# Attention, then two MoE layers, on one core: a unit's scores behind the preceding unit's values, and a last phase on three pairs of 512 tokens

## The chip, the core and the metric

The kernel runs on one core of one Trainium2 chip. A time is the device time of one execution in microseconds (us). TensorE (PE in the profile) does the matrix products, VectorE (DVE) and ScalarE (ACT) element-wise work, GpSimd (POOL) some of the same, and SyncE (SP) issues DMA transfers. PEld is the loading of TensorE's stationary operand; SPq is SP's instruction queue.

## What is computed

The inputs are float64 where the weights are concerned and float32 else. Attention over chunks of 32 queries: each chunk sees 16 tokens to its left, itself, 8 to its right, and 8 memory tokens. Behind it stand two feed-forward layers over 3072 tokens of width 512.

```python
for c in range(768 // 32):
    q_c = q[:, :, 32 * c:32 * c + 32]                       # 4 x 8 heads, 64 wide
    k_full = concat([mem_k, k[:, :, max(0, 32 * c - 16):32 * c + 40]])
    v_full = concat([mem_v, v[:, :, max(0, 32 * c - 16):32 * c + 40]])
    a = softmax(q_c @ k_full.T / 8)
    out[:, :, 32 * c:32 * c + 32] = a @ v_full
x = out.transpose(0, 2, 1, 3).reshape(3072, 512)
h = x @ w_in                                                # 512 -> 2048
x = (max(h, 0) + log1p(exp(-abs(h)))) @ w_out               # 2048 -> 512
return ((x @ w_a) * (x @ w_b)) @ w_o2                       # 512 -> 1536 -> 512
```

## The kernel before

**Products in three parts.** Every float32 operand of a wide product is kept as a high and a low part; a product is high x high, high x low and low x high, added up in PSUM. That makes three matmuls of each.

**First layer: 8 tiles of TT = 384 tokens.** A tile runs 16 blocks f of the hidden width. `emit_h` (L531) makes ph, 12 matmuls of 384 columns, in one of two PSUM banks of tag h. `emit_soft` (L543) forms the softplus: three ScalarE operations on e (L545 abs, L546 exp, L547 ln), one VectorE operation g (L549), then `split` into g_h and g_l. `emit_x1` (L555), two blocks later (LAG = 2), adds g times the second weight into four PSUM banks acc0 to acc3, 12 matmuls px. At a tile's end the four sums are copied and stored into x1_scratch.

**Attention in between.** 128 tokens with all heads are a unit; three units make a tile, and they are done while the tile before runs. Units 0 to 2 (tile 0) are done as blocks of 64 tokens ahead of everything, units 3 to 5 by a way of their own (EARLY_STEPS). Units u = 6 to 23, which the change touches, go through these steps of `class Unit` (L393):

- `turn` (L403): three VectorE transposes (L410, L412, L413) that bring the loaded keys kn and queries qn into kt and qt, and two small ScalarE copies of the memory keys into kt; for the first unit of a batch (u = 6, 12, 18) a small transpose of the memory keys ahead.
- `scores` (L417): 16 small float32 matmuls sc, which the profile shows as 32, into the two banks of tag att.
- `soft` (L432): maximum on VectorE, exponentials on ScalarE. `norm` (L440): the division, mostly on GpSimd.
- `flip` and `flip2` (L443): five VectorE transposes each, pieces 0 and 1 and then pieces 2 and 3 of af.
- `values` (L468): 16 such matmuls pxa, again 32 in the profile, the first half on pieces 0 and 1, the second on pieces 2 and 3, into one bank of tag att.
- `place` (L479): the result split into the x of the next tile, by ScalarE and VectorE (L484).

**What sets the order.** A table gives each step a place in slots, relative to the unit's place; two slots are one block f. `att_at(slot)` (L899) runs all steps that are due: at an even slot 2f behind ph and the softplus of block f, at an odd one behind the px matmuls. In tiles 1 to 6 the order of SP, TensorE and VectorE is the written one, ScalarE and GpSimd are ordered by a scheduler; in tile 0 and from tile 7 all are as written. Each instruction waits by semaphores for the data and for the free buffer it needs.

```python
STEPS = ((-8, "turn"), (-5.2, "scores"), (-4.9, "soft"), (-3, "norm"), (-0.9, "flip"), (1.1, "flip2"),
         (3, "values"), (3.1, "place"))
at = 2 * NF1 * (i + 1) // UPT - START + NEXT_LATER * (i == EARLY) - (i % UPT == UPT - 1)
plan += [(at + d - steps[-1][0], i, getattr(unit, step)) for d, step in steps]
```

The last unit of a tile (u = 8, 11, 14, 17, 20, 23) stands one slot earlier; `Loaded.fetch` (L184, issues L187 and L189), which loads the next tile's keys and queries in 4 parts of 8 or more DMAs, is planned 1 to 4 slots behind that unit's `turn`. Between these steps the raw weights of the second MoE are loaded and put together on VectorE (`Early`, val L640 and L641) and stored into v_scratch (L644).

**Last phase: the second layer on 4 pairs of 2 x 384 tokens.** For each of 12 blocks f, `pair_step` (L767) forms (x w_a) and (x w_b) of both halves by seven block products (Strassen's way: PRODUCTS = 11, s2, s3, s1, 12, 22, s4, on sums of quarters of x that `add_pair` makes), each product six matmuls of 384 columns (`product`, L720) into the banks pX, pY, pW, pV. VectorE adds and multiplies the results into c1 and c2, ScalarE and VectorE split them, and `job` (L739) multiplies 128 tokens of them with w_o2: six matmuls py of 512 columns, three jobs in a step. The sums of x are split into high and low by `split_hi` and `split_lo`, those of the first pair on VectorE during tile 7, those of the others during the preceding pair, mostly in its last step. From the second pair on, the weights' sums u are reloaded from u_scratch.

## Time and profile before

| what | value |
| --- | --- |
| median of three runs | 1189.16 us (1187.32 to 1193.07) |
| profiled execution, span of its instructions | 1185.4 us (its own time outside the span is not given) |
| TensorE busy | 1177.1 us, 99%, 7966 matmuls |
| loading of its operands | 1115.2 us, 94%, beside the matmuls |
| VectorE busy | 734.8 us, 62%, 1707 instructions |
| ScalarE busy | 537.0 us, 45%, 1329 instructions |
| GpSimd busy | 279.5 us, 24%, 249 instructions |

The profiled execution is one execution; its span ends 3.8 us below the median of the three timed runs. In the timeline, a row is a run of equal instructions: its start in us from the span's start, the time from its first start to its last end, the engine, the line, the operation, the tiles written and read with the shape, and the number of instructions. What stands in brackets is idle time of the engine ahead of it, and what ended it. Matmuls overlap, so the time that a group of them takes is read from its start to the start of the next group.

### The profile page before, as it was taken

Reading aid. Unit: us, or ns where it says so; the run is one execution under the profiler, and the core shown is the slowest. Engines: PE = TensorE matmul, PEld = TensorE weight load, DVE = VectorE, ACT = ScalarE, POOL = GpSimd, SP = SyncE. Lnnn points to the kernel's source line nnn. Section 1 sums busy time; section 2 is a strip of 40 time slices with the busy share of each in tenths; the row PEclk is TensorE's granted clock in tenths of the full one; section 3 lists DMA queues with packets and bytes.
Section 4 is the critical chain, followed back from the end, with each engine's and each line's share of the span. In section 5 each row is a group of like instructions: output and inputs, shape, how many; then the busy total and the mean of one; then the engine's idle time right before and its main releaser. Section 6 shows DMA issues by size and latency. Waiting matters only on the chain.

```text
span 1185.4 us, 21520 instructions
## 1 busy us (share of the span) xinstructions
PE 1177.1 (99%) x7966; PEld 1115.2 (94%) x7966; DVE 734.8 (62%) x1707; ACT 537.0 (45%) x1329; POOL 279.5 (24%) x249
## 2 busy tenths in 40 slices
PE   9999999999999999999999999999999999999998
PEld 7899999999999999999999999999999999999997
DVE  6888654555556555465387668755666456655565
ACT  6899565655656566565564433221112211212010
POOL 2000323223232222322325778200211002100000
PEclk9999999999999999999999999999999999999999
DMA  9955334353343633432556895788554965379521
GB/s 237 295 178 111 109 86 110 93 115 107 87 107 93 120 107 84 104 97 62 178 205 238 324 341 190 267 327 298 199 196 141 375 234 183 133 255 369 194 80 54
DMA packets 198841, 209.86 MB, mean 177 GB/s; under 512 B 121632, under 2 KB 150224, under 8 KB 198736
## 3 DMA queue, kind: packets, MB, share of 16 engines
q1 hardware_dynamic: 198352, 208.43, 54.9%
q8 instruction: 63, 1.03, 0.4%
q14 instruction: 42, 0.34, 0.1%
q0 software_dynamic: 384, 0.05, 0.0%
HBM read 158.11 MB, written 50.33 MB: 176 GB/s over the span
## 4 chain that ended last, share of the span: by engine, by line
PE 93%; ACT 3%; DVE 2%; DMA 1%; issue 1%; SPq 0%; DVEq 0%; ACTq 0%
PE ph L538 21%; PE px L562 21%; PE py L749 17%; PE pW L726 8%; PE pX L726 8%; PE pV L726 8%; PE pY L726 4%; PE pxa L476 2%; PE sc L429 1%; DMA raw<-in_moe_w_in_dram 1%; DVE tmp L122 1%; ACT sm L383 1%; DMA vv<-in_v_dram 0%; ACT work L383 0%; DVE tmp L121 0%
## 5 line engine op out<-in xcount | busy, mean ns | idle before, releaser
L538 PE MATMUL ph<-x,w 128*128 128x384 f32 x1536 | 289.7, 336 | 0.1
L538 PEld LDWEIGHTS ph<-x,w 128*128 128x128 f32 x1536 | 266.7, 188 | 2.2 <-issue 0.3
L749 PE MATMUL py<-w2o,c 128*128 128x512 f32 (+1 forms) x870 | 222.2, 392 | 0.0
L549 DVE SCALAR_TENSOR_TENSOR g<-ph,e 128x384 f32<-128x384 f32 x128 | 71.3, 557 | 205.6 <-ACT e L547 205.3
L749 PEld LDWEIGHTS py<-w2o,c 128*128 128x128 f32 x870 | 160.5, 188 | 25.3
L808 ACT CAST c<-c 128x384 fp32r<-128x384 f32 x48 | 24.7, 514 | 302.4 <-DVE c L806 269.8
L726 PE MATMUL pX<-x,u 128*128 128x384 f32 x576 | 115.5, 334 | 0.0
L758 DVE TENSOR_TENSOR y<-py,y 128x512 f32<-128x512 f32 (+1 forms) x121 | 83.0, 686 | 47.3 <-PE py L749 46.9
L545 ACT ACTIVATE e<-ph 128x384 f32<-128x384 f32 x128 | 62.3, 486 | 103.9 <-PE ph L538 89.9
L726 PEld LDWEIGHTS pX<-x,u 128*128 128x128 f32 x576 | 102.1, 188 | 4.1
L447 DVE STREAM_TRANSPOSE af<-sm 32x256 f32<-32x256 f32 x180 | 78.2, 435 | 2.5
L804 DVE TENSOR_TENSOR d<-pW,q 128x384 f32<-128x384 f32 x48 | 26.7, 557 | 68.5 <-PE pW L726 68.5
L546 ACT ACTIVATE e<-e 128x384 f32<-128x384 f32 x128 | 67.3, 526 | 4.0
L547 ACT ACTIVATE e<-e 128x384 f32<-128x384 f32 x128 | 67.3, 526 | 3.8
L383 ACT ACTIVATE sm<-sm,st 128x96 f32<-128x96 f32 x168 | 60.5, 362 | 3.6 <-DVE st L379 3.6
L818 ACT CAST c<-c 128x384 fp32r<-128x384 f32 x48 | 24.6, 513 | 77.9 <-DVE c L816 76.9
L726 PE MATMUL pW<-xs,u 128*128 128x384 f32 x288 | 57.8, 335 | 0.0
L726 PE MATMUL pV<-xx,u 128*128 128x384 f32 x288 | 57.8, 335 | 0.0
L726 PE MATMUL pV<-xs,u 128*128 128x384 f32 x288 | 57.6, 334 | 0.0
L726 PE MATMUL pY<-xs,u 128*128 128x384 f32 x288 | 57.6, 334 | 0.0
L726 PE MATMUL pW<-xx,u 128*128 128x384 f32 x288 | 57.6, 334 | 0.0
L726 PEld LDWEIGHTS pV<-xx,u 128*128 128x128 f32 x288 | 51.5, 188 | 4.1
(251 smaller groups left out, 2229.3 us busy)
## 6 DMA issues: line engine op xcount, KB each, us to landing
u<-u_scratch SPq DMA_DIRECT2D x108, 512.0 KB
u_scratch<-u SPq DMA_DIRECT2D x36, 512.0 KB
w2o<-w2o_scratch SPq DMA_DIRECT2D x36, 512.0 KB
u<-u_scratch SPq DMA_DIRECT2D x36, 256.0 KB
raw<-in_moe_w_in_dram SPq DMA_DIRECT2D x16, 512.0 KB
raw<-in_moe_w_out_dram SPq DMA_DIRECT2D x16, 512.0 KB
vn<-in_v_dram SPq DMA_DIRECT2D x35, 176.0 KB
raw_a<-in_moe_w_a_dram SPq DMA_DIRECT2D x12, 512.0 KB
```

The costliest lines, as they stand in the source:

```text
L383: nc.scalar.activation(sm[:, h], sm[:, h], AF.Exp, bias=st[:, 0, h:h + 1], scale=-1.0, accum_out=st[:, 1, h:h + 1])
L447: nc.vector.transpose(out=af[32 * kb:32 * kb + 32, x], in_=self.sm[32 * x:32 * x + 32, :, 32 * kb:32 * kb + 32])
L538: nc.tensor.matmul(ph, lhsT=w[:, a, kt * P:(kt + 1) * P], rhs=x[:, c, kt, :], start=n == 0, stop=n == 3 * KT - 1)
L545: nc.scalar.activation(e, ph, AF.Abs)
L546: nc.scalar.activation(e, e, AF.Exp, scale=-1.0)
L547: nc.scalar.activation(e, e, AF.Ln, bias=1.0)
L549: nc.vector.scalar_tensor_tensor(g, ph, 0.0, e, ALU.max, ALU.add)
L562: nc.tensor.matmul(acc[t][i][:, :TT], lhsT=a, rhs=c, start=f == 0 and m == 0, stop=f == NF1 - 1 and m == 2)
L726: nc.tensor.matmul(bank[:, :TT], lhsT=u[:, j, a, kt * P:kt * P + P], rhs=x[:, c, kt, :], start=first_ and m == 0, stop=m == 3 * KH - 1, sk ...
L749: nc.tensor.matmul(b, lhsT=c[:, x, r], rhs=w[:, y, cols], start=n == 0, stop=n == 3 * GROUP - 1)
L758: tt(y, b, y, ALU.add)
L804: tt(d21, w[:, :TT], q, ALU.add)
```

## The change

- The table of steps becomes two, HEAD and TAIL. The scores of a unit from u = 7 on stand 0.1 slot ahead of the place of the preceding unit, that is directly behind its values; for u = 6 they stand 8.3 slots ahead of its own place (HEAD_AT). `turn` stands 2.8 slots, `soft` 0.11 and `norm` 2.2 from the scores. `flip` and `flip2` stand 4 and 2 slots ahead of the place, `values` 0.1 ahead, as before. First units of a tile (u = 6, 9, 12, ...) have their turn 0.5 later and their flips 1 earlier, as before.
- The values of u = 6 to 23 go into a bank of tag h instead of att (`own_bank`).
- The last phase works on three pairs of 2 x 512 tokens (T2 = 512, NPAIR = 3): a product is six matmuls of 512 columns; each two blocks leave eight jobs, no longer six, and a step has places for four, no longer three. x1_scratch is laid out for any width.
- To make room, g, g_h and g_l of the first layer share one tile each (`turn_of`), the operands of the block products find homes in buffers of the first layer (`operand`, `pieces_of`), and `pair_step` adds and multiplies in place.
- The splits of products 22 and s4 of the first pair move from tile 7 into the first step of the phase; those of the later pairs move into the last step of the pair before, and the low part of s4 into the first step of the pair itself.

```diff
@@ -16,12 +16,14 @@
 
 NEG = -1.0e30
 TT = 384
+T2 = 512
 
 LAG = 2
-STEPS = ((-8, "turn"), (-5.2, "scores"), (-4.9, "soft"), (-3, "norm"), (-0.9, "flip"), (1.1, "flip2"),
-         (3, "values"), (3.1, "place"))
+HEAD = ((-2.8, "turn"), (0, "scores"), (0.11, "soft"), (2.2, "norm"))
+TAIL = ((-4, "flip"), (-2, "flip2"), (-0.1, "values"), (0, "place"))
+HEAD_AT = -8.3
+FIRST_LATER = {"turn": 0.5, "flip": -1, "flip2": -1}
 START = 1.7
-FIRST_STEPS = tuple((d + {"turn": 0.5, "flip": -1, "flip2": -1}.get(step, 0), step) for d, step in STEPS)
...
@@ -468,7 +471,7 @@
         def values(self):
             u = self.u
             vn = self.v.v
-            self.px = px = ps.tile([P, 512], F32, tag="att", name=f"pxa{u}").rearrange("p (i t) -> p i t", i=KT)
+            self.px = px = ps.tile([P, 512], F32, tag="h" if self.own_bank else "att", name=f"pxa{u}").rearrange("p (i t) -> p i t", i=KT)
...
@@ -497,19 +500,26 @@
     units = [Unit(u) for u in range(B * NU)]
 
     plan = []
+    placed = None
     for i, unit in enumerate(units[UPT:]):
         at = 2 * NF1 * (i + 1) // UPT - START + NEXT_LATER * (i == EARLY) - (i % UPT == UPT - 1)
-        steps = FIRST_STEPS if i % UPT == 0 else STEPS
         if i < EARLY:
             steps = EARLY_STEPS[i]
             at = steps[-1][0]
-        plan += [(at + d - steps[-1][0], i, getattr(unit, step)) for d, step in steps]
+        else:
+            unit.own_bank = True
+            scored = at + HEAD_AT if i == EARLY else placed - 0.1
+            later = FIRST_LATER if i % UPT == 0 else {}
+            steps = [(scored + d + later.get(step, 0), step) for d, step in HEAD]
+            steps += [(at + d + later.get(step, 0), step) for d, step in TAIL]
+        placed = at
+        plan += [(d, i, getattr(unit, step)) for d, step in steps]
         if i < SETS:
             plan.append((2 + i, -1, unit.load_v))
         if i + SETS < len(units[UPT:]):
             plan.append((at + 1, i, units[UPT + i + SETS].load_v))
         if i % UPT == UPT - 1 and unit.u + 1 < len(units):
-            turned = at + steps[0][0] - steps[-1][0]
+            turned = steps[0][0]
             plan += [(turned + 1 + part, i, partial(loaded.fetch, unit.u // UPT + 1, part)) for part in range(KT)]
     plan += [(at, -1, lambda i=i: packed[1].turn(i)) for i, at in enumerate(PACKED_AT)]
...
@@ -519,10 +529,18 @@
     gt = {}
     acc = {}
     anchor = [None]
+    rings, n_turn = {}, {}
+
+    def turn_of(tag, n, dtype):
+
+        if tag not in rings:
+            rings[tag] = mp.tile([P, n, TT], dtype, tag=tag, name=tag, bufs=1)
+            n_turn[tag] = 0
+        n_turn[tag] += 1
+        return rings[tag][:, n_turn[tag] % n]
 
     def split(val, name, engine=nc.gpsimd, between=None):
-        hi = mp.tile([P, TT], F32R, tag="gh", name=name + "h", bufs=3)
-        lo = mp.tile([P, TT], F32R, tag="gl", name=name + "l", bufs=3)
+        hi, lo = turn_of("gh", 3, F32R), turn_of("gl", 3, F32R)
...
@@ -579,36 +597,56 @@
 
     def load_pair(p):
         for n, (t, k) in {"11": (0, 0), "12": (0, 1), "21": (1, 0), "22": (1, 1)}.items():
-            raws[n] = wp.tile([P, KH, TT], F32, tag="w", name=f"x{n}_{p}")
-            nc.sync.dma_start(raws[n], x1d[2 * p + t, :, KH * k:KH * k + KH, :])
+            raws[n] = wp.tile([P, KH, T2], F32, tag="w", name=f"x{n}_{p}")
+            c0 = (2 * p + t) * T2
+            nc.sync.dma_start(raws[n], x1d[:, KH * k:KH * k + KH, c0:c0 + T2])
...
 
+    def operand(p, n):
+
+        def home(key, pool, shape, tag):
+            if (p, key) not in parts:
+                parts[p, key] = pool.tile(shape, F32R, tag=tag, name=f"{key}_{p}", bufs=2 if tag == "x" else 1)
+            return parts[p, key]
+
+        if n in ("11", "s2", "s3"):
+            return [home(f"x{n}", late["x"], [P, KH, 2, T2], f"x{n}")]
+        if n == "s1":
+            return [home("xs1a", late["x"], [P, 1, 2, T2], "xs1"), home("xa", mp, [P, 3, 2, T2], "x")[:, 0:1]]
+        if n == "12":
+            return [home("xa", mp, [P, 3, 2, T2], "x")[:, 1:3]]
+        if n == "22":
+            return [home("xb", mp, [P, 3, 2, T2], "x")[:, 0:2]]
+        return [parts[p, "xb"][:, 2:3], home("xs4b", mp, [P, 1, 2, T2], "gh")]
+
+    def pieces_of(p, n):
+        k = 0
+        for x in sums[p, n]:
+            yield x, raws[n][:, k:k + x.shape[1]]
+            k += x.shape[1]
+
     def split_hi(p, n, copy):
-        if n in ("22", "s4"):
-            if (p, "2") not in parts:
-                parts[p, "2"] = mp.tile([P, 2, 2, KH, TT], F32R, tag="x", name=f"xx{p}")
-            sums[p, n] = parts[p, "2"][:, n == "s4"]
-        else:
-            sums[p, n] = late["x"].tile([P, 2, KH, TT], F32R, tag="s", name=f"x{n}_{p}")
-        copy(sums[p, n][:, 0], raws[n])
+        sums[p, n] = operand(p, n)
+        for x, raw in pieces_of(p, n):
+            copy(x[:, :, 0], raw)
 
     def split_lo(p, n, engine):
-        x = sums[p, n]
-        engine.tensor_tensor(x[:, 1], raws[n], x[:, 0].bitcast(F32), ALU.subtract)
+        for x, raw in pieces_of(p, n):
+            engine.tensor_tensor(x[:, :, 1], raw, x[:, :, 0].bitcast(F32), ALU.subtract)
...
@@ -719,11 +757,12 @@
 
     def product(bank, p, f, n, first_):
         i, j = PLACE[n]
-        u, x = us[p, f][i], sums[p, n]
+        u = us[p, f][i]
+        x = [part[:, k] for part in sums[p, n] for k in range(part.shape[1])]
         m = 0
         for kt in range(KH):
             for a, c in ((0, 0), (0, 1), (1, 0)):
-                nc.tensor.matmul(bank[:, :TT], lhsT=u[:, j, a, kt * P:kt * P + P], rhs=x[:, c, kt, :],
+                nc.tensor.matmul(bank[:, :T2], lhsT=u[:, j, a, kt * P:kt * P + P], rhs=x[kt][:, c],
                                  start=first_ and m == 0, stop=m == 3 * KH - 1, skip_group_check=True)
                 m += 1
...
@@ -767,60 +806,58 @@
     def pair_step(p, f, at, between=()):
 
         late_lo = pair_step.late
+        last = (p, f) == (NPAIR - 1, NF2 - 1)
         x = bank("h", f"pX{p}_{f}")
         product(x, p, f, "11", True)
-        s = temp("e", f"s{p}_{f}")
-        nc.scalar.copy(s, x[:, :TT])
+        q = temp("e", f"q{p}_{f}")
+        nc.scalar.copy(q, x)
...
-        r = temp("e", f"r{p}_{f}")
-        tt(r, w[:, :TT], q, ALU.add)
+        r = temp("g", f"r{p}_{f}")
+        tt(r, w, q, ALU.add)
         at(2)
         if between:
             between[1]()
+        else:
+            next_job()
         v = bank("acc0", f"pV{p}_{f}")
         product(v, p, f, "s1", True)
-        d22 = temp("gl", f"d22_{p}_{f}")
-        tt(d22, v[:, :TT], r, ALU.add)
+        tt(r, v, r, ALU.add)
         at(3)
         if not between:
...
         if f % GROUP == GROUP - 1:
-            jobs.extend((p, f // GROUP, half, i) for half in (1, 0) for i in range(TT // P))
+            jobs.extend((p, f // GROUP, half, i) for half in (1, 0) for i in range(T2 // P))
...
-        for n in PRODUCTS:
+        for n in PRODUCTS[:5]:
             pieces.append(partial(split_hi, 0, n, nc.vector.tensor_copy))
             pieces.append(partial(split_lo, 0, n, nc.vector))
         for k, piece in enumerate(pieces):
-            plan2.setdefault(16 + 2 * k // 3, []).append(piece)
+            plan2.setdefault(16 + k, []).append(piece)
...
-        for p in range(NTILE // 2):
-            more = p + 1 < NTILE // 2
+        for p in range(NPAIR):
+            more = p + 1 < NPAIR
...
-                        if f == 9 and k in (1, 3):
-                            n = "22" if k == 1 else "s4"
-                            split_hi(p + 1, n, nc.scalar.copy)
-                            split_lo(p + 1, n, nc.gpsimd)
                         if f == NF2 - 1:
-                            if k < 5:
-                                split_hi(p + 1, PRODUCTS[k], nc.scalar.copy)
-                            if 0 < k < 6:
+                            split_hi(p + 1, PRODUCTS[k], nc.scalar.copy)
+                            if k > 0:
                                 split_lo(p + 1, PRODUCTS[k - 1], nc.gpsimd if k in (2, 4) else nc.vector)
+                    if f == 0 and k == 0 and p > 0:
+                        split_lo(p, PRODUCTS[6], nc.vector)
+                    if p == f == 0 and k in (0, 2):
+                        split_hi(0, PRODUCTS[5 + k // 2], nc.scalar.copy)
+                    if p == f == 0 and k in (1, 3):
+                        split_lo(0, PRODUCTS[5 + k // 2], nc.vector)
 
```

What moves on VectorE in tile 3, from the g of block 8 on: u = 13 is the middle unit, u = 14 the one behind it. af, sm: its flips (L447, L450 after); kt14, qt14: the turn of u = 14; val_b: raw weights; x4 with pxa13: its place. Before:

```order
L549 SCALAR_TENSOR_TENSOR g3_8_3993<-ph3_8_3976,e3_8_3989 128x384
L447 STREAM_TRANSPOSE af_83<-sm13_3901 32x256 x5
L640 TENSOR_SCALAR val_b4_4017<-raw_b4_3935 128x512
L641 SCALAR_TENSOR_TENSOR val_b4_4017<-raw_b4_3935,val_b4_4017 128x512
L549 SCALAR_TENSOR_TENSOR g3_9_4040<-ph3_9_4023,e3_9_4036 128x384
L447 STREAM_TRANSPOSE af_83<-sm13_3901 32x256 x5
L410 STREAM_TRANSPOSE kt14_4063<-kn_78 128x8x64
L412 STREAM_TRANSPOSE kt14_4063<-kn_78 128x8x32
L413 STREAM_TRANSPOSE qt14_4064<-qn_79 128x512
L549 SCALAR_TENSOR_TENSOR g3_10_4087<-ph3_10_4070,e3_10_4083 128x384
L484 TENSOR_TENSOR x4_3814<-pxa13_4093,x4_3814 128x4x128
```

And with the change (g_660 is the shared tile of g):

```order
L567 SCALAR_TENSOR_TENSOR g_660<-ph3_8_3805,e3_8_3818 128x384
L450 STREAM_TRANSPOSE af_83<-sm13_3676 32x256 x5
L413 STREAM_TRANSPOSE kt14_3843<-kn_78 128x8x64
L415 STREAM_TRANSPOSE kt14_3843<-kn_78 128x8x32
L416 STREAM_TRANSPOSE qt14_3844<-qn_79 128x512
L678 TENSOR_SCALAR val_b4_3850<-raw_b4_3770 128x512
L679 SCALAR_TENSOR_TENSOR val_b4_3850<-raw_b4_3770,val_b4_3850 128x512
L567 SCALAR_TENSOR_TENSOR g_660<-ph3_9_3856,e3_9_3869 128x384
L450 STREAM_TRANSPOSE af_83<-sm13_3676 32x256 x5
L567 SCALAR_TENSOR_TENSOR g_660<-ph3_10_3913,e3_10_3926 128x384
L487 TENSOR_TENSOR x4_3670<-pxa13_3933,x4_3670 128x4x128
```

The turn of u = 14 (three transposes) moves from behind the second flip of u = 13 to directly behind its first flip, ahead of val_b, the g of block 9 and the second flip.

TensorE at the same place, from ph of block 10 on. pxa13: values of u = 13; sc0_14, sc1_14: scores of u = 14; px: the second product of block 8. Before:

```order
L538 MATMUL ph3_10_4070<-x3_2926,w18_1161 128x384 x12
L476 MATMUL pxa13_4093<-af_83,vn0_82 64x64 x16
L562 MATMUL px3_0_3692<-g3_8h_3995,w19_1216 128x384
L562 MATMUL px3_0_3692<-g3_8l_3996,w19_1216 128x384
...
L562 MATMUL px3_3_3695<-g3_8h_3995,w19_1216 128x384
L429 MATMUL sc0_14_4150<-kt14_4063,qt14_4064 64x96 x2
L429 MATMUL sc1_14_4151<-kt14_4063,qt14_4064 64x96 x2
```

With the change:

```order
L556 MATMUL ph3_10_3913<-x3_2832,w18_1143 128x384 x12
L479 MATMUL pxa13_3933<-af_83,vn0_82 64x64 x16
L432 MATMUL sc0_14_3950<-kt14_3843,qt14_3844 64x96 x2
L432 MATMUL sc1_14_3951<-kt14_3843,qt14_3844 64x96 x2
...
L580 MATMUL px3_0_3536<-gh_666,w19_1195 128x384
L580 MATMUL px3_0_3536<-gl_667,w19_1195 128x384
```

The scores of u = 14 move from behind the twelve px of block 8 to directly behind the values of u = 13. The ph of block 11 stands behind all of them in both.

VectorE in the last third of tile 3, where u = 14 is the last unit of its tile and u = 15 the first of the next (kt15, qt15: its turn). Before:

```order
L549 SCALAR_TENSOR_TENSOR g3_13_4293<-ph3_13_4276,e3_13_4289 128x384
L447 STREAM_TRANSPOSE af_83<-sm14_4200 32x256 x5
L549 SCALAR_TENSOR_TENSOR g3_14_4333<-ph3_14_4316,e3_14_4329 128x384
L447 STREAM_TRANSPOSE af_83<-sm14_4200 32x256 x5
L549 SCALAR_TENSOR_TENSOR g3_15_4373<-ph3_15_4356,e3_15_4369 128x384
L484 TENSOR_TENSOR x4_3814<-pxa14_4379,x4_3814 128x4x128
L410 STREAM_TRANSPOSE kt15_4398<-kn_78 128x8x64
L412 STREAM_TRANSPOSE kt15_4398<-kn_78 128x8x32
L413 STREAM_TRANSPOSE qt15_4399<-qn_79 128x512
```

With the change:

```order
L567 SCALAR_TENSOR_TENSOR g_660<-ph3_13_4090,e3_13_4103 128x384
L450 STREAM_TRANSPOSE af_83<-sm14_3970 32x256 x5
L413 STREAM_TRANSPOSE kt15_4127<-kn_78 128x8x64
L415 STREAM_TRANSPOSE kt15_4127<-kn_78 128x8x32
L416 STREAM_TRANSPOSE qt15_4128<-qn_79 128x512
L567 SCALAR_TENSOR_TENSOR g_660<-ph3_14_4134,e3_14_4147 128x384
L450 STREAM_TRANSPOSE af_83<-sm14_3970 32x256 x5
L567 SCALAR_TENSOR_TENSOR g_660<-ph3_15_4171,e3_15_4184 128x384
L487 TENSOR_TENSOR x4_3670<-pxa14_4191,x4_3670 128x4x128
```

The turn of u = 15 moves from behind the place of u = 14 to directly behind its first flip.

## Rows read from the trace of the kernel before

**Rows 1.** The page, sections 1 and 2, all engines and the granted clock

```profile
PE 1177.1 (99%) x7966; PEld 1115.2 (94%) x7966; DVE 734.8 (62%) x1707; ACT 537.0 (45%) x1329; POOL 279.5 (24%) x249
...
PEclk9999999999999999999999999999999999999999
```

**Rows 2.** Timeline of TensorE, last phase: start, us, engine, line, op, out<-in

```profile
803.32 1.20 PE L726 MATMUL pW<-xx,u 128*128 128x384 f32 x6
804.36 1.55 PE L749 MATMUL py<-w2o,c 128*128 128x512 f32 x6
805.75 1.21 PE L726 MATMUL pV<-xx,u 128*128 128x384 f32 x6
```

**Rows 3.** Timeline of TensorE, values of u = 12 and u = 13

```profile
287.85 1.15 PE L476 MATMUL pxa<-af,vn 96*64 96x64 f32 x32
...
310.87 2.24 PE L538 MATMUL ph<-x,w 128*128 128x384 f32 x12
313.05 1.22 PE L476 MATMUL pxa<-af,vn 96*64 96x64 f32 x32
314.20 0.45 PE L562 MATMUL px<-g_8h,w 128*128 128x384 f32 x1
314.48 0.34 PE L562 MATMUL px<-g_8l,w 128*128 128x384 f32 x1
...
317.51 2.35 PE L538 MATMUL ph<-x,w 128*128 128x384 f32 x12
```

**Rows 4.** Timeline of TensorE, scores of u = 14 and u = 15

```profile
316.49 1.09 PE L429 MATMUL sc<-kt,qt 64*64 64x96 f32 x32
...
344.04 0.89 PE L429 MATMUL sc<-kt,qt 64*64 64x96 f32 x32
```

**Rows 5.** Timeline of VectorE, flips of u = 13, turn of u = 14

```profile
307.28 2.22 DVE L447 STREAM_TRANSPOSE af<-sm 32x256 f32<-32x256 f32 x5
...
310.70 0.56 DVE L549 SCALAR_TENSOR_TENSOR g<-ph,e 128x384 f32<-128x384 f32 x1
311.29 2.24 DVE L447 STREAM_TRANSPOSE af<-sm 32x256 f32<-32x256 f32 x5
313.56 0.71 DVE L410 STREAM_TRANSPOSE kt<-kn 128x512 f32<-128x512 f32 x1
...
314.52 0.67 DVE L413 STREAM_TRANSPOSE qt<-qn 128x512 f32<-128x512 f32 x1
315.49 0.56 DVE L549 SCALAR_TENSOR_TENSOR g<-ph,e 128x384 f32<-128x384 f32 x1 [0.30 <-ACT e L547]
```

**Rows 6.** Timelines of VectorE and TensorE, first flip and values of u = 20

```profile
477.38 0.56 DVE L549 SCALAR_TENSOR_TENSOR g<-ph,e 128x384 f32<-128x384 f32 x1 [2.90 <-ACT e L547]
477.85 2.22 DVE L447 STREAM_TRANSPOSE af<-sm 32x256 f32<-32x256 f32 x5
...
483.88 1.11 PE L476 MATMUL pxa<-af,vn 96*64 96x64 f32 x28
```

**Rows 7.** Timeline of VectorE, flip of u = 14, turn of u = 15

```profile
330.67 2.22 DVE L447 STREAM_TRANSPOSE af<-sm 32x256 f32<-32x256 f32 x5
334.09 0.56 DVE L549 SCALAR_TENSOR_TENSOR g<-ph,e 128x384 f32<-128x384 f32 x1 [1.20 <-ACT e L547]
...
339.32 0.70 DVE L410 STREAM_TRANSPOSE kt<-kn 128x512 f32<-128x512 f32 x1
```

**Rows 8.** Timeline of SP's queue (SPq), loads of keys and queries for tile 5

```profile
310.79 0.34 SPq L626 DMA_DIRECT2D raw_o<-in_moe_w_out_dram  x1
...
314.62 0.33 SPq L187 DMA_DIRECT2D kn<-in_k_dram  x1
...
326.50 0.91 SPq L644 DMA_DIRECT2D v_scratch<-val_o  x1
...
335.78 0.47 SPq L189 DMA_DIRECT2D qn<-in_q_dram  x1
```

**Rows 9.** Windows, 337.5 to 338: busy of each engine, clock, DMA share, GB/s

```profile
337.50:338.00 0.50, 0.50 (x8) 0.43 (x5) 0.00 (x0) 0.47 (x2) 0.00 (x0) 1.00 0.00 0
```

More of the change, by code (lines that the diff above doesn't have):

```diff
@@ L547, in emit_soft @@
         nc.scalar.activation(e, e, AF.Ln, bias=1.0)
-        g = mp.tile([P, TT], F32, tag="g", name=f"g{t}_{f}")
+        g = turn_of("g", 2, F32)
         nc.vector.scalar_tensor_tensor(g, ph, 0.0, e, ALU.max, ALU.add)
@@ L568, in emit_x1 @@
                 else:
-                    o = mp.tile([P, TT], F32, tag=OUT_TAGS[i], name=f"xo{t}_{i}")
+                    o = turn_of("g", 2, F32) if i > 1 else mp.tile([P, TT], F32, tag="e", name=f"xo{t}_{i}")
                 nc.vector.tensor_copy(o, acc[t][i][:, :TT])
-                nc.sync.dma_start(x1d[t, :, i, :], o)
+                nc.sync.dma_start(x1d[:, i, TT * t:TT * t + TT], o)
             del acc[t]
@@ L587, in add_pair @@
         if n == "s1":
-            r[n] = wp.tile([P, KH, TT], F32, tag="w", name="xs1")
+            r[n] = wp.tile([P, KH, T2], F32, tag="w", name="xs1")
             engine.tensor_tensor(r[n], r["21"], r["22"], ALU.add)
         elif n == "s2":
-            r[n] = wp.tile([P, KH, TT], F32, tag="w", name="xs2")
+            r[n] = wp.tile([P, KH, T2], F32, tag="w", name="xs2")
             engine.tensor_tensor(r[n], r["s1"], r["11"], ALU.subtract)
@@ L733, in temp @@
     def temp(tag, name):
-        return mp.tile([P, TT], F32, tag=tag, name=name, bufs=3 if tag in ("gh", "gl") else 2)
+        return mp.tile([P, T2], F32, tag=tag, name=name, bufs=2 if tag == "e" else 1)
     cs, yacc, jobs, n_jobs = {}, {}, [], [0]
@@ L750, in job @@
                 n += 1
-        place = 3 * (1 - half) + i
+        place = T2 // P * (1 - half) + i
         if m == 0:
@@ L759, in job @@
             if m == NF2 // GROUP - 1:
-                r0 = (2 * p + half) * TT + i * P
+                r0 = (2 * p + half) * T2 + i * P
                 nc.sync.dma_start(out[r0:r0 + P, cols], y)
@@ L776, in pair_step @@
         product(y, p, f, "s2", True)
-        q = temp("gh", f"q{p}_{f}")
-        tt(q, y[:, :TT], s, ALU.add)
+        tt(q, y, q, ALU.add)
         while late_lo:
@@ L783, in pair_step @@
             between[0]()
-        elif (p, f) != (NTILE // 2 - 1, NF2 - 1):
+        elif not last:
             next_job()
@@ L802, in pair_step @@
         product(w, p, f, "22", False)
-        d21 = temp("e", f"d21_{p}_{f}")
-        tt(d21, w[:, :TT], q, ALU.add)
-        c2 = temp("gl", f"c2_{p}_{f}")
-        tt(c2, d21, d22, ALU.mult)
-        cs[p, f, 1] = cc = wp.tile([P, 2, TT], F32R, tag="w", name=f"c{p}_{f}_1")
-        nc.scalar.copy(cc[:, 0], c2)
+        d21 = temp("gl", f"d21_{p}_{f}")
+        tt(d21, w, q, ALU.add)
+        tt(r, d21, r, ALU.mult)
+        cs[p, f, 1] = cc = wp.tile([P, 2, T2], F32R, tag="w", name=f"c{p}_{f}_1")
+        nc.scalar.copy(cc[:, 0], r)
         at(5)
@@ L928, in order @@
                 ctx.enter_context(tc.manual_schedule(engines={mybir.EngineType.SP, *engines.values()}))
[L929 removed]
+                late["x"] = ctx.enter_context(tc.tile_pool(name="late", bufs=1))
             for f in range(NF1):
@@ L970, in at @@
                     nxt = (p, f + 1) if f + 1 < NF2 else (p + 1, 0)
-                    if nxt[0] > 0 and nxt[0] < NTILE // 2:
+                    if nxt[0] > 0 and nxt[0] < NPAIR:
                         if k < 4:
```

24 lines of the change are left out of this document (11 added, 13 removed).

## The prediction, made before the changed kernel had run

> **What bounds the kernel now.** I read the page first. TensorE is busy for 1177.1 of 1185.4 us and its granted clock is full (2.4 GHz, shown as 9 tenths and more) in every slice [rows 1]. So a matmul group that becomes shorter is gained whole, and any wait put ahead of TensorE is lost whole; VectorE at 62% and ScalarE at 45% count only where TensorE waits for them. Next the timeline of TensorE, in the two stages that the change touches. In the last phase, six products of 384 columns take 1.04 us and the six of a job with 512 columns 1.39 us, with no gap between groups [rows 2]. In tiles 1 to 6 a unit's two small groups stand alone between wide ones. The wide group ph starts at 310.87; at 1.04 us for six its twelve would end at 312.95, but the values begin at 313.05. Behind them the first wide matmul takes 0.28 us (314.20 to 314.48) where 0.17 is usual [rows 3]. Each visit to small matmuls thus costs 0.10 us on the way in and 0.11 on the way out.
>
> Then the timeline of VectorE before the values of a middle unit (u = 13). First flip, val_b, g, second flip follow each other without idle time from 307.28 to 313.53, and only then comes the turn of u = 14 [rows 5]. The second 16 of the 32 value matmuls read pieces 2 and 3 of af, which the second flip writes; TensorE wants them at about 313.5. It already waits a little: 1.22 us for the group, against 1.15 in u = 12 [rows 3]. VectorE has no slack at this place.
>
> **The change, part by part.** Durations are from the one profiled execution, span 1185.4 us; the median of the three runs, 1189.16, is 3.8 us more, and I add the sum to that.
>
> *Products of 512 columns.* 4 x 12 x 7 = 336 groups of six become 3 x 12 x 7 = 252. At 1.04 that is 349.4 us, at 1.39 350.3. The wide group costs four thirds of the narrow one, so nothing is saved; I take 0, and +-0.01 us of reading per group gives bounds of -2.5 and +2.5. The jobs keep number and width. VectorE's and ScalarE's operations in the phase handle as many elements in fewer instructions. The second MoE's weights are loaded again for two pairs, no longer three, so the DMA load falls. Both splits moved into the first step (22 and s4) have three to four product groups of 1.39 us ahead of their use: nothing.
> The six-matmul rows show no fixed cost per matmul. The Trainium skill (TensorE: Matmul & The Clock Gate, section "Wait — 56ns, not 53.3ns?") gives each warm matmul a fixed 2.5 ns beside its columns; by it, as an estimate, 504 matmuls fewer would save 1.3 us, and the sum below would be 6.9 instead of 8.2 us.
>
> *Scores behind values.* 17 units (u = 7 to 23) join the preceding unit's visit; u = 6 stays alone. Saved is one way in and one way out, 0.21 us [rows 3]. The step from the last value to the first score is not in the trace. It may cost another 0.11 (the dearer of the two ways), or the scores may slide in for less than the ordinary step of 0.17 that a wide matmul takes: 0.10 to 0.38. I take 0.23, near the two measured ways: -3.9 us, bounds -1.7 and -6.5.
> Three of the 18 score groups now take 1.09 us where 0.89 is usual [rows 4]. The values' bank of tag att comes free only when place has ended, and the scores need it; with the values in a bank of tag h this goes: -0.6.
>
> *The turn in the middle units (u = 7, 10, 13, 16, 19, 22).* The table puts turn at 2.8 slots ahead of the scores, and the scores now stand at the preceding unit's values. So u = 14's turn lands between u = 13's two flips, ahead of val_b, g and the second flip. It takes 1.63 us (313.56 to 315.19) [rows 5]. Since nothing idles between there and the second flip, that flip ends 1.63 later and TensorE waits for it with sc, x1 and all later groups behind it. A part comes back. In u = 13 the first flip starts 5.77 us ahead of the values; in u = 20, where ScalarE has no exponentials at that moment, it starts 6.03 ahead [rows 6]. With the softmax up to three slots earlier I expect 6.03 everywhere, so 0.26 is regained: 1.37 x 6 = +8.2 us, bounds 7 and 9.8 (nothing regained).
>
> *The turn in the last units (u = 8, 11, 14, 17, 20; u = 23 has none behind it).* Here there is no val between, and g waits 1.20 us for ScalarE [rows 7], which covers part of the turn. But ScalarE's two copies into kt, which wait for the turn, now stand between exp and ln of this g. Behind u = 13 they do so today: g starts at 315.49, 1.96 us after the flip's end at 313.53 [rows 5]. From u = 14's first flip, ending at 332.89 less 0.26, that gives 334.59 against 334.09: 0.50 us late.
> Also, this turn reads the next tile's keys and queries. SP issues them from 314.62 to 335.78, and DMA is quiet from 337.5 [rows 8, 9]; today's turn comes at 339.3, behind place, and never waits. After the change SP's weight load (310.79, behind val_b) moves 1.37 later, so the first key load, two issues of about 0.4 behind (this load's and a store's), goes out at about 310.79 + 1.37 + 0.83 = 312.99, 1.63 earlier than now. The store at 326.50 (0.96 us) moves behind them. So the last issue is at 333.2, landed 1.7 later, at 334.9. The turn wants the data at 332.63, plus the 1.37 that TensorE lost at u = 13: 334.0. Keys, one issue earlier, are due some 0.4 us late. So 0.5 to 1.4 us per unit; I take 0.9, half the lateness of the last landing: +4.5 us, bounds 2.5 and 7.
> In first units the turn falls between the second flip and g, 3 slots ahead of the values: nothing.
>
> *The h bank.* Values now sit between ph(f) and ph(f+1) in the rotation of two banks, so ph(f+1) waits for g(f), one ph earlier than today. Behind u = 13, g ends at 316.05, later by 1.6 with the turn ahead; ph(f+1) starts at 317.51 and moves by the same stall plus 0.8 to 1 us, for the scores now stand ahead of it too: nothing, with about a microsecond to spare.
>
> **Sum.** 0 - 3.9 - 0.6 + 8.2 + 4.5 = +8.2 us, bounds -0.1 and +16.2 when all ends fall together. 1189.16 + 8.2 = **1197.4 us**, a span of about 1193.6.
>
> **Rivals.**
> *The flips are in time (not slower).* Place: VectorE between the two flips. If the first flip began 7.4 us or more ahead of the values, where it begins 5.8 ahead now, the turn would fit and only the savings would stay: -4.5, 1184.7 us. For it: the softmax is done up to three slots earlier. Against: VectorE works in its written order, the first flip stands behind a g that waits 2.90 us for ScalarE even where the softmax is long past [rows 6], and this g hangs on a ph at a fixed place. Chance 0.17.
> *The next tile's loads come much later.* If SP gains nothing from the earlier turn, the loads land at 337.5 against a want at 334.0, and the last units lose 2 us more each than in my sum at most; at 1.5 us that is +7.5: 1204.9 us. For: the loads go out one by one over 21 us, and a store among them took twice the usual half microsecond to issue [rows 8]. Against: the first is held today only by the turn. Chance 0.12.
> *A new wait in the last phase.* At the two changes of pair, ScalarE's split of s1 waits for product 12 and that of 22 for product s4, with copies that the steps need queued behind. 3 us at each would make 1203.4. Against: TensorE has 8 to 10 us of other groups between the split and its use, and one change of pair fewer. Chance 0.06.
>
> **How the numbers follow.** My forecast has the remaining 0.65; its own range is 1193 to 1202. A measurement of this kernel tells some 0.5% (5.9 us) from no change, so faster means under 1183.2 and slower over 1195.1. Of the forecast about 0.47 lies above 1195.1 and 0.18 between; the two dear rivals add 0.17 above and 0.01 between; the cheap one splits into 0.08 faster and 0.09 same. Faster 0.08, same 0.28, slower 0.64. The range 1185 to 1206 leaves out half of the cheap rival and the dear ends, less than 0.2.
>
> **What would show it.** In the waits of TensorE, pxa waiting for af of VectorE, six times about 1.3 us and five times 0.5 to 1.5, which the page of before does not have; pxa groups of about 2.5 us in middle units; the order flip, turn, val, g, flip on VectorE without idle time; kt waiting for a key DMA in the last units. Score groups directly behind the values, one gap of 0.28 less per unit. In the last phase 15.3 us per step (seven groups and four jobs at 1.39) and no waits. I am wrong if pxa stays at 1.2 us, or if six products take clearly less than 1.39 us, or if TensorE waits in the last phase.

## The result and the profile after

The changed kernel takes 1204.44 us (median of 6 runs, 1201.62 to 1206.79) against 1189.89 for the kernel before (6 runs, 1187.32 to 1193.56): a ratio of 1.012, 95% interval 1.0098 to 1.0142. It is slower by 14.6 us, where the prediction said 8.2. The stretch ahead of the first values takes 67.4 to 72.3 us in the nine profiled executions (TensorE's waits for the first queries are 0.2 to 3.0 us, and in three of them the granted clock is 0.50 for 3.4 or 6.8 us), so below the stages behind that point are compared; where two kernels share the code of a stage they agree to 0.1 us. The profiled execution of the changed kernel is the slowest of its six (1206.79 us), and each ledger below is that of one execution.

The page of the changed kernel, sections 1 and 2, answers to [rows 1]:

```profile
PE 1175.2 (98%) x7462; PEld 1059.7 (88%) x7462; DVE 728.1 (60%) x1603; ACT 534.1 (44%) x1293; POOL 264.5 (22%) x239
...
PEclk9899998999989999999999999999999999999999
```

TensorE is busy 1175.2 of 1205.0 us: its busy time shrank by 2 us and the span grew by 20. The granted clock, full everywhere before, is down three times in the attention stage, for 6.8 us each: twice the row shows it as a digit 8, the third time it is spread over two slices and hidden in the 9s (from 512 to 516 us the granted clock is 0.50). The first 8 of the row lies in the first 70 us. The waits of TensorE (engine, what, for whom; us in total, times, longest us), the rows that the page of before did not have:

```profile
PE pxa L479 <- DVE af L450: 14.2, 11, 1.6
PE pxa L479 <- DVE g L567: 5.4, 5, 1.8
```

Eleven waits for the flips and five for a g, both at the values; one of the five, 0.30 us, stands at the first unit u = 6, the others in last units. Split at the first value matmul of u = 3 and at the first product matmul pX, and ended with the last matmul, the profiled executions give (us):

| kernel | up to the values of u = 3 | attention and first layer | last phase |
| --- | --- | --- | --- |
| before | 67.7 | 559.9 | 554.3 |
| changed | 71.9 | 586.6 | 543.1 |
| only the pairs of 512 | 69.3 | 559.9 | 543.1 |
| only the attention | 68.6 | 585.7 | 554.3 |
| turn ahead of the first flip | 70.0 | 559.4 | 543.1 |
| first units alone | 67.9 | 566.5 | 543.1 |
| both repairs | 68.1 | 560.9 | 543.1 |
| turns far ahead | 72.3 | 579.2 | 543.1 |
| before, jobs together | 67.4 | 559.9 | 552.8 |

So the change loses 26.7 us in the attention stage, not 8, and wins 11.2 in the last phase, where the prediction had 0.

**The middle units.** TensorE at the values of u = 13 (start, us, engine, line, operation, count, in brackets the idle time ahead):

```profile
324.45 2.25 PE L556 MATMUL ph<-x,w 128*128 128x384 f32 x12
326.63 0.69 PE L479 MATMUL pxa<-af,vn 96*64 96x64 f32 x16
328.36 0.69 PE L479 MATMUL pxa<-af,vn 96*64 96x64 f32 x16 [1.04 <-DVE af L450]
328.98 0.89 PE L432 MATMUL sc<-kt,qt 64*64 64x96 f32 x32
329.80 0.44 PE L580 MATMUL px<-gh,w 128*128 128x384 f32 x1
```

And VectorE ahead of it, which answers to [rows 5]:

```profile
320.60 2.22 DVE L450 STREAM_TRANSPOSE af<-sm 32x256 f32<-32x256 f32 x5
322.83 0.71 DVE L413 STREAM_TRANSPOSE kt<-kn 128x512 f32<-128x512 f32 x1
...
323.79 0.67 DVE L416 STREAM_TRANSPOSE qt<-qn 128x512 f32<-128x512 f32 x1
...
325.49 0.55 DVE L567 SCALAR_TENSOR_TENSOR g<-ph,e 128x384 f32<-128x384 f32 x1
326.07 2.23 DVE L450 STREAM_TRANSPOSE af<-sm 32x256 f32<-32x256 f32 x5
```

The order is as predicted: flip, turn (322.83 to 324.46), val_b, g, second flip, without idle time. The first flip starts 6.03 us ahead of the values (320.60 to 326.63), the figure the prediction took from u = 20. The second half of the values then waits 1.04 us. The whole visit, from the last wide matmul ahead to the third behind, less three ordinary steps of 0.173, is 3.37 us; without the turn between the flips it is 2.18 (the run with the turn ahead, below). The scores follow the values without a gap.

**The last units.** VectorE at u = 14, which answers to [rows 7]:

```profile
344.79 2.22 DVE L450 STREAM_TRANSPOSE af<-sm 32x256 f32<-32x256 f32 x5
349.31 0.71 DVE L413 STREAM_TRANSPOSE kt<-kn 128x512 f32<-128x512 f32 x1 [2.30 <-DMA kn<-in_k_dram]
...
351.25 0.56 DVE L567 SCALAR_TENSOR_TENSOR g<-ph,e 128x384 f32<-128x384 f32 x1 [0.31 <-ACT e L565]
351.84 2.23 DVE L450 STREAM_TRANSPOSE af<-sm 32x256 f32<-32x256 f32 x5
```

The turn finds its keys missing and stands 2.30 us; the g behind it starts 6.46 us after the first flip's start, where it started 3.42 after it before. The same wait is 3.14, 1.52 (for the queries), 2.10 and 2.97 us for u = 8, 11, 17 and 20. ScalarE shows why g doesn't slip past (exp, the two copies of the memory keys into kt, ln):

```profile
347.29 0.53 ACT L564 ACTIVATE e<-e 128x384 f32<-128x384 f32 x1
350.38 0.34 ACT L418 COPY kt<-mem_t 128x32 f32<-128x32 f32 x2 [2.57 <-DVE kt L415]
350.63 0.52 ACT L565 ACTIVATE e<-e 128x384 f32<-128x384 f32 x1
```

The copies wait for the turn, and the logarithm that g needs stands behind them. SP's queue, which answers to [rows 8]:

```profile
326.46 0.42 SPq L189 DMA_DIRECT2D kn<-in_k_dram  x1
...
347.72 0.47 SPq L191 DMA_DIRECT2D qn<-in_q_dram  x1
348.29 0.41 SPq L682 DMA_DIRECT2D v_scratch<-val_o  x1
```

and TensorE at the same values:

```profile
351.86 0.69 PE L479 MATMUL pxa<-af,vn 96*64 96x64 f32 x16 [0.97 <-DVE g L567]
354.13 1.13 PE L479 MATMUL pxa<-af,vn 96*64 96x64 f32 x16 [1.58 <-DVE af L450]
355.18 1.56 PE L432 MATMUL sc<-kt,qt 64*64 64x96 f32 x32
356.67 0.69 PE L580 MATMUL px<-gh,w 128*128 128x384 f32 x1
357.16 0.52 PE L580 MATMUL px<-gl,w 128*128 128x384 f32 x1
```

Two waits: the values first want the bank of tag h that the late g still holds (0.97 us), then the second flip (1.58 us). And then the next thing: px steps of 0.32 us where 0.17 is usual. The windows of this stretch (us, length; busy of TensorE, its loads, VectorE, ScalarE, GpSimd; then the granted clock, DMA share, GB/s) show it:

```profile
348.00:351.00 3.00, 2.89 (x17) 2.57 (x15) 1.63 (x3) 0.62 (x3) 0.00 (x0) 1.00 0.50 129
...
357.00:360.00 3.00, 3.00 (x10) 3.00 (x10) 1.29 (x16) 2.92 (x16) 0.38 (x1) 0.50 0.72 203
361.00:364.00 3.00, 3.00 (x19) 3.00 (x18) 0.00 (x0) 0.90 (x2) 0.00 (x0) 1.00 0.02 5
```

The granted clock is 1.00 up to the waits, 0.50 (1.2 GHz) behind them and 1.00 again from 361. It fell behind the visits of u = 8, 14 and 20, whose two waits add up to 2.5 us and more, and not behind u = 11 and 17, whose waits add up to 1.69 and 2.25. This is no threshold: the run with the attention alone, below, has a fall behind less.

**The ledger of the attention stage**, from the lengths of the visits as measured above: six middle visits +5.2 us against the two visits that each replaces; six first units -0.8; five last visits 29.4 against 11.9, +17.5; and some 33 wide matmuls at half clock behind three of these, +4.8. Sum 26.7.

**The last phase**, which answers to [rows 2]:

```profile
804.21 1.52 PE L788 MATMUL py<-w2o,c 128*128 128x512 f32 x6
805.57 1.52 PE L765 MATMUL pW<-xs,u 128*128 128x512 f32 x6
806.93 1.52 PE L788 MATMUL py<-w2o,c 128*128 128x512 f32 x6
```

Groups of six start every 1.36 us, products and jobs alike. A job took 1.39 before.

### The profile page after: what moved, and what is told of

The parts are those of the page before. It is cut to its first block, busy times and chain, and to the rows that moved or that the text cites. A ratio compares the mean times of both kernels' runs of the same rounds, so it can differ in the third digit from the quotient of the medians.

```text
span 1205.0 us, 20110 instructions
## 1 busy us (share of the span) xinstructions
PE 1175.2 (98%) x7462; PEld 1059.7 (88%) x7462; DVE 728.1 (60%) x1603; ACT 534.1 (44%) x1293; POOL 264.5 (22%) x239
## 4 chain that ended last, share of the span: by engine, by line
PE 82%; DVE 6%; SPq 5%; DMA 4%; ACT 2%; issue 2%; DVEq 0%; ACTq 0%
PE px L580 17%; PE ph L556 16%; PE py L788 16%; PE pX L765 8%; PE pW L765 8%; PE pV L765 8%; PE pY L765 4%; DVE af L450 3%; SPq L189 2%; PE pxa L479 2%; SPq L191 2%; PE sc L432 1%; DMA kp<-in_k_dram 1%; DVE g L567 1%; DMA raw<-in_moe_w_in_dram 1%
## 5 line engine op out<-in xcount | busy, mean ns | idle before, releaser
L580 PE MATMUL px<-gh,w 128*128 128x384 f32 x1024 | 286.2, 340 | 0.0
L580 PEld LDWEIGHTS px<-gh,w 128*128 128x128 f32 x1024 | 190.0, 191 | 2.2 <-issue 0.9
L580 PE MATMUL px<-gl,w 128*128 128x384 f32 x512 | 173.6, 339 | 0.0
L547 POOL TENSOR_TENSOR gl<-g,gh 128x384 fp32r<-128x384 f32 x96 | 98.3, 1025 | 219.1 <-ACT gh L544 218.6
L544 ACT CAST gh<-g 128x384 fp32r<-128x384 f32 x128 | 65.8, 514 | 77.5 <-DVE g L567 76.3
L580 PEld LDWEIGHTS px<-gl,w 128*128 128x128 f32 x512 | 97.8, 191 | 0.8 <-POOL gl L547 0.7
L450 DVE STREAM_TRANSPOSE af<-sm 32x256 f32<-32x256 f32 x180 | 78.2, 434 | 2.5
L844 DVE TENSOR_TENSOR d<-pW,q 128x512 f32<-128x512 f32 x36 | 24.9, 691 | 68.9 <-PE pW L765 68.9
L765 PE MATMUL pX<-x,u 128*128 128x512 f32 x216 | 54.8, 389 | 0.0
L765 PE MATMUL pW<-xs,u 128*128 128x512 f32 x216 | 54.8, 389 | 0.0
L765 PE MATMUL pY<-xs,u 128*128 128x512 f32 x216 | 54.8, 389 | 0.0
```

Source lines behind the costliest of these rows:

```text
L450: nc.vector.transpose(out=af[32 * kb:32 * kb + 32, x], in_=self.sm[32 * x:32 * x + 32, :, 32 * kb:32 * kb + 32])
L544: anchor[0] = nc.scalar.copy(hi, val)
L547: engine.tensor_tensor(lo, val, hi.bitcast(F32), ALU.subtract)
L580: nc.tensor.matmul(acc[t][i][:, :TT], lhsT=a, rhs=c, start=f == 0 and m == 0, stop=f == NF1 - 1 and m == 2)
L765: nc.tensor.matmul(bank[:, :T2], lhsT=u[:, j, a, kt * P:kt * P + P], rhs=x[kt][:, c], start=first_ and m == 0, stop=m == 3 * KH - 1, skip_ ...
```

## Experiments

Two theories on the loss (the turn between the flips, and the next tile's keys) and two on the gain were put to the chip. Ratios are to the kernel before, run on the same chip.

**Only the pairs of 512.** The changed kernel with the table of steps and the bank of the values of before:

```diff
-HEAD = ((-2.8, "turn"), (0, "scores"), (0.11, "soft"), (2.2, "norm"))
-TAIL = ((-4, "flip"), (-2, "flip2"), (-0.1, "values"), (0, "place"))
+STEPS = ((-8, "turn"), (-5.2, "scores"), (-4.9, "soft"), (-3, "norm"), (-0.9, "flip"), (1.1, "flip2"),
+         (3, "values"), (3.1, "place"))
...
-            unit.own_bank = True
```

> Only the last phase of the change (three pairs of 512 tokens); the attention steps stand as before, with the values in a bank of tag att. Theory A, from the trace of the changed kernel, where six matmuls of 512 columns take 1.36 us in products and jobs alike: 252 product groups at 1.36 instead of 336 at 1.04 give -6.7 us, and 144 job groups at 1.36 instead of 1.39 give -4.2: about 11 us faster than before, near 1179. Rival B, the prediction's term of 0 for the products: no change, 1190.

Measured: 1176.42 us (1175.82 to 1177.58), ratio 0.9872 (0.9845 to 0.9898). The last phase is 543.1 as in the changed kernel, the attention stage 559.9 as before. Theory A holds: 11.2 us in the last phase, and the prediction's term of 0 falls. The medians differ by more, 15.3 us, since that of the kernel before is 1191.68 in this round; the rest is not seen in these two stages. The shared tiles of g, which this kernel keeps, cost the first layer nothing.

**Only the attention.** The kernel before with the change's table of steps and bank; the last phase stays:

```diff
-STEPS = ((-8, "turn"), (-5.2, "scores"), (-4.9, "soft"), (-3, "norm"), (-0.9, "flip"), (1.1, "flip2"),
-         (3, "values"), (3.1, "place"))
+HEAD = ((-2.8, "turn"), (0, "scores"), (0.11, "soft"), (2.2, "norm"))
+TAIL = ((-4, "flip"), (-2, "flip2"), (-0.1, "values"), (0, "place"))
...
+            unit.own_bank = True
+            scored = at + HEAD_AT if i == EARLY else placed - 0.1
```

> Only the steps of the attention are changed (scores behind the preceding unit's values, own bank for the values); the last phase stays on four pairs of 384. Theory A: the changed kernel lost about 26 us here and won 11 in the last phase, so this is slower than before by about 26, near 1216, with the same waits as the changed kernel: six of about 1.3 us for the second flip in the middle units, five of 1.5 to 3.5 in the last units, and a granted clock that falls to half for 6.8 us behind some of these. Rival B, the prediction's own terms without a gain in the last phase: +8, 1198.

Measured: 1214.79 us (1213.88 to 1216.99), ratio 1.0198 (1.0173 to 1.0223); attention stage 585.7, 25.8 us over before. The waits of TensorE:

```profile
PE pxa L478 <- DVE af L449: 14.1, 11, 1.6
PE pxa L478 <- DVE g L558: 4.9, 5, 1.8
```

The loss lies wholly in the attention's steps, and by the stages the two parts add up: 25.8 lost here and 11.2 won above, where the changed kernel has 26.7 and 11.2. By the medians they do not: +23.1 here and -15.3 above make +7.8, against the 14.6 measured together; the medians take in the first 70 us, which the stages leave out. The six waits of the middle units are 1.04 us each, not 1.3. Here the granted clock fell to 0.50 behind all five last units, but for 3.4 us each instead of 6.8 for three. At u = 11 it fell behind one wait:

```profile
272.33 0.69 PE L478 MATMUL pxa<-af,vn 96*64 96x64 f32 x16 [1.53 <-DVE af L449]
...
274.00:276.50 2.50, 2.50 (x12) 2.50 (x9) 1.79 (x17) 1.98 (x12) 1.01 (x1) 0.50 0.43 99
```

The changed kernel kept a full clock behind 0.67 and 1.58 us at u = 17. So the length of the waits alone does not tell whether the clock falls.

**The turn of the last unit ahead of the first flip.**

```diff
+            sooner = {"turn": -1.8} if i % UPT == UPT - 1 else {}
-            steps = [(scored + d + later.get(step, 0), step) for d, step in HEAD]
+            steps = [(scored + d + later.get(step, 0) + sooner.get(step, 0), step) for d, step in HEAD]
```

> The changed kernel, but the turn of a tile's last unit stands 1.8 slots earlier, so in the middle units' visits it lies ahead of the first flip, in VectorE's idle time ahead of g, and no longer between the flips. Nothing else is moved; the loads of the next tile's keys and queries, which wait for this turn, start about 4 us earlier. Theory A: the six waits of 1.3 us go (-7.6 us), and VectorE's waits of 2.1 to 2.3 us for the keys in the last units go too, since they come from the late start of the loads; what stays there is a turn between the flips, 0.3 to 0.6 us each: near 1183. Rival B: the loads are slow by themselves, so the last units wait as long as in the changed kernel: only -7.6, near 1197.

Measured: 1178.04 us (1174.54 to 1178.53), ratio 0.988 (0.9854 to 0.9907). The attention stage is 559.4, 27.2 less than in the changed kernel. The middle visits are 2.18 us, so the whole loss there was the turn's place. And VectorE at u = 14:

```profile
331.93 2.22 DVE L450 STREAM_TRANSPOSE af<-sm 32x256 f32<-32x256 f32 x5
334.17 0.71 DVE L413 STREAM_TRANSPOSE kt<-kn 128x512 f32<-128x512 f32 x1
...
336.11 0.56 DVE L568 SCALAR_TENSOR_TENSOR g<-ph,e 128x384 f32<-128x384 f32 x1 [0.31 <-ACT e L566]
336.70 2.23 DVE L450 STREAM_TRANSPOSE af<-sm 32x256 f32<-32x256 f32 x5
```

No wait for keys: the turn follows the flip at once, because the loads started earlier. It was by more than the expected 4 us: the first load goes out 8.6 to 9.1 us ahead of the middle unit's values, where the changed kernel has 0.1 to 0.2. The second half of the values then waits 0.33 us, and the clock does not fall in this stage. Theory A holds, and its time was too high by 5: the falls of the clock, which it left out of the sum, went as well.

**The first units alone.**

```diff
-            scored = at + HEAD_AT if i == EARLY else placed - 0.1
+            scored = at + HEAD_AT if i % UPT == 0 else placed - 0.1
```

> The changed kernel, but the first unit of each tile has its turn and scores at their old place, ahead of its own values and apart from the preceding unit's, so nothing of the next tile stands in a last unit's visit. Theory A: the five last units lose nothing any more (12 us of waits, and the falls of the clock behind them, some 7 to 10 us), while five units stand apart again (+1); the six waits of 1.3 us in the middle units stay: near 1186. Rival B: the clock falls because of the waits in the middle units as well, so it goes on falling and only the waits go: near 1194.

Measured: 1184.75 us (7 runs, 1182.38 to 1187.2), ratio 0.9947 (0.9927 to 0.9967). The waits of TensorE:

```profile
PE pxa L479 <- DVE af L450: 6.2, 6, 1.0
...
PE px L580 <- POOL gl L547: 0.9, 3, 0.3
```

The six waits of the middle units stay, alone, and the mean granted clock of the profiled execution is 1.000. So these six single waits of 1.04 us did not bring the clock down; in the changed kernel it fell behind last units only. Theory A holds. A small new wait shows, px for gl of GpSimd.

**Both repairs together** (the two edits above).

> The changed kernel with both repairs: the turn of a tile's last unit 1.8 slots earlier, ahead of the first flip, and the first unit of each tile with turn and scores at their old place. Theory: no wait of TensorE for af or g in units 7 to 23; a joined visit is 0.20 us shorter than two (2.11 against 1.285 + 1.025), 12 units are joined, and three waits for the bank of tag att go: 3 us under the run with the pairs alone (1176.4), near 1173.5. Rival: the turn ahead of the first flip delays that flip, so some 0.3 us a unit are lost again in the middle units: 1175.5.

Measured: 1177.03 us (1176.04 to 1181.16), ratio 0.9906 (0.9883 to 0.9929), no better than the pairs alone, and the attention stage is 560.9, 1 us longer than before. Theory and rival both miss. The visits are as short as expected, but TensorE now has these waits:

```profile
PE px L581 <- POOL gl L548: 1.2, 4, 0.3
...
PE ph L557 <- DVE g L568: 0.4, 1, 0.4
```

and GpSimd at the first of them shows the softmax's division (L392) directly ahead of two gl that TensorE is about to need:

```profile
224.71 1.47 POOL L392 TENSOR_TENSOR sm<-sm,st 128x768 f32<-128x768 f32 x1 [7.48 <-DVE st L390]
226.13 2.16 POOL L548 TENSOR_TENSOR gl<-g,gh 128x384 fp32r<-128x384 f32 x2
```

In the changed kernel the division stands ahead of two gl as well, but it starts 10.17 us behind the start of the values of u = 9, here 10.64, and TensorE loses under 0.2 us there; why it comes later here was not tried. With the slower steps around them the stalls of this kernel come to some 3.5 us (560.9 with 2.5 saved, against 559.9), and eat what the visits save.

**The jobs of a step in one place**, in the kernel before:

```diff
-        elif (p, f) != (NTILE // 2 - 1, NF2 - 1):
-            next_job()
...
         at(3)
         if not between:
             next_job()
+            next_job()
+            if (p, f) != (NTILE // 2 - 1, NF2 - 1):
+                next_job()
...
         at(5)
-        if not between:
-            next_job()
```

> The kernel before, with the three jobs of a step of the last phase in one place, ahead of product 12, instead of one in each of three places. Theory A, on why a job's six matmuls of 512 columns took 1.39 us among products of 384 and take 1.36 among products of 512: the extra 0.03 us belongs to the change between the two widths, so the second and third job of a row cost 1.36: 2 x 0.029 x 46 = 2.7 us less in the last phase, 544.5 instead of 547.2. Rival B: it belongs to the layout of the operand c (rows of 384), so nothing changes in the jobs, 547.2. In both the order of the products' results is the same; three jobs in a row may also let VectorE or ScalarE come late for product 12, which the waits of TensorE would show.

Measured: 1186.17 us (10 runs, 1185.17 to 1190.71), ratio 0.9976 (0.9959 to 0.9992); the last phase is 552.8 where the kernel before has 554.3 by the same cut: -1.5. (The expectation named the two as 544.5 and 547.2 by a cut at the last px, a little further on.)

```profile
901.61 4.28 PE L749 MATMUL py<-w2o,c 128*128 128x512 f32 x18
905.73 1.23 PE L726 MATMUL pX<-x,u 128*128 128x384 f32 x6
906.79 0.68 PE L726 MATMUL pW<-xx,u 128*128 128x384 f32 x3
```

Eighteen job matmuls take 4.12 us, 1.37 per job; the first job of a row takes 1.389, the second 1.372, and the third 1.360 like those of the changed kernel. The operand's layout is the same as before, so rival B falls: the extra time belongs to the change of width. The gain was below theory A's because the second job is not yet at 1.360, and the product behind three jobs takes 1.066 where the one behind a single job took 1.044: a part of the extra time moved there.

**All turns outside the flips.**

```diff
+            sooner = {"turn": (-2.3, 0, -5.8)[i % UPT]} if i > EARLY else {}
-            steps = [(scored + d + later.get(step, 0), step) for d, step in HEAD]
+            steps = [(scored + d + later.get(step, 0) + sooner.get(step, 0), step) for d, step in HEAD]
```

> The changed kernel with all scores behind the preceding values, but the turn of a tile's last unit 5.8 slots earlier and that of a tile's first unit 2.3 slots earlier, so that every turn lies outside the two flips and the loads of the next tile's keys and queries start some 12 us earlier than in the changed kernel. Theory: 17 joined visits at 0.20 us and three waits for the bank of tag att make 4 us under the run with the pairs alone, and no waits of TensorE for af or g: near 1172.5. Rival: the turn of the next tile's first unit, now wanted 4.8 us earlier, still finds its keys missing (the loads take 24 us on SP's queue), so that the flips of the last units come late as in the changed kernel: five units lose 1 to 3 us each, 1178 to 1188.

Measured: 1196.44 us (7 runs, 1192.06 to 1204.1), ratio 1.0066 (1.0038 to 1.0094). Neither came: the keys are there in time, but three of the middle units (u = 7, 16, 19) now lose what the last ones lost, with visits of 6.6, 8.2 and 7.6 us, and the clock fell behind each. VectorE and SP's queue at u = 16:

```profile
391.94 2.22 DVE L450 STREAM_TRANSPOSE af<-sm 32x256 f32<-32x256 f32 x5
398.93 0.43 DVE L679 TENSOR_SCALAR val_a<-raw_a 128x512 uint32<-128x512 uint32 x1 [4.77 <-DMA raw_a<-in_moe_w_a_dram]
...
400.25 0.55 DVE L568 SCALAR_TENSOR_TENSOR g<-ph,e 128x384 f32<-128x384 f32 x1
```

```profile
383.49 0.32 SPq L189 DMA_DIRECT2D kn<-in_k_dram  x1
...
394.57 0.42 SPq L668 DMA_DIRECT2D raw_a<-in_moe_w_a_dram  x1
```

The loads of keys and queries follow their turn, so they now stand ahead of a raw weight's load in SP's queue. That load goes out at 394.57 behind 11 us of them; val_a waits 4.77 us for it, g and the second flip stand behind val_a, and the values behind these. At u = 10 and 13 a val waits as long (5.69 and 6.52 us), but behind the visit; u = 10 loses 0.89 us to its second flip.

## Why the prediction came out as it did

The time lies in the stated range of 1185 to 1206, and the sign is right. But it lies above 1193 to 1202, the range that the prediction gave its own forecast, and that the sum came so near is luck, by two errors that partly cancel: a gain of 11.2 us that it did not have, and 18.5 us of loss more than it had in the attention (26.7 against 8.2). Its upper bound is also added up wrongly: its terms at their dear ends make +17.0, not +16.2.

- **Products of 512 columns, 0 us: wrong.** The failed step is "The wide group costs four thirds of the narrow one, so nothing is saved". The 1.39 us was read at jobs that stand between narrow groups, and 0.029 of it belongs to the change of width. At 226.7 ns a matmul of 512 and 173.3 one of 384 columns there is a fixed part of 13.3 ns (53.3 ns for 128 columns more). 504 matmuls fewer give -6.7 us; 144 jobs at 1.36 instead of 1.39 give -4.2; together -10.9 of the 11.2 measured. The prediction's "six-matmul rows show no fixed cost" was read from two groups, of which one was not clean. By its own sign, "six products take clearly less than 1.39 us", this term failed: they take 1.36, and a step with seven groups and four jobs is 15.0 us, not 15.3. The Trainium skill (TensorE: Matmul & The Clock Gate, section "Wait — 56ns, not 53.3ns?"), which the prediction set against its row, was right that a matmul has a fixed part; for these matmuls the traces give 13.3 ns where it states some 2.5.
- **Scores behind values, -3.9 us: right.** A joined visit without waits is 2.11 us against 1.285 + 1.025: 0.20 per unit, taken as 0.23. The three waits for the bank of tag att are gone: 0.6, as taken.
- **Middle units, +8.2 us: right in kind, a little high.** 3.37 against 2.18 us, 1.19 per unit and 7.1 in all; TensorE waits in exactly the six visits named, and the run with the turn ahead takes it away.
- **Last units, +4.5 us: the mechanism was there, the size was not.** Two steps failed. "Keys, one issue earlier, are due some 0.4 us late": they were 1.5 to 3.1 late. Taken back by the 13.6 us that u = 13's values had moved, the first load went out at 312.9, as predicted (312.99), but the want came at 333.4 (said 334.0) and the data at 335.7 (said 334.9, less one issue): from first to last the loads took 21.7 us on SP's queue, as before, though the store of val_o no longer stood among them but behind (348.29): single issues that took up to 1.55 us, where 0.47 is usual, made up for it. And "The h bank": the text looked at ph(f+1) and found a microsecond to spare, while the one that waits for the late g is the values' own bank. What the values would have done in the bank of tag att was not tried. Five visits cost 18.5 us more than undisturbed joined ones would, 3.7 each, not 0.9.
- **The clock: missing from the sum.** The page of before shows it full everywhere, and no term asked what waits of TensorE do to it: +4.8 us in the wide matmuls, and a part of the five visits.
- **The rivals.** That the loads come late (0.12) is what happened in kind, at 2 us beyond the sum's assumption; its 1204.9 lies near the measured time, though only because the last phase paid back 11. The wait in the last phase did not show: no row of TensorE's waits lies there.

The lowest median of these is that of the pairs alone: 1176.42 us, ratio 0.9872 (0.9845 to 0.9898); by the last phase alone it is 11.2 us, 0.9%. The run with the turn ahead, 0.988 (0.9854 to 0.9907), can't be told from it. The joined visits, repaired in two ways, gave 0.5 us in the stage at best (559.4 against 559.9).
